# Raw pieces of w_in by half the rows, and five buffers for q, k and v, in a kernel of attention, a dense layer and a mixture of experts

## The chip, the cores and the metric

The kernel runs on one core of a Trainium2 chip. The metric is the time of one execution on the device, in microseconds (us). TensorE (PE) multiplies, VectorE (DVE) and ScalarE (ACT) work on elements, GpSimd (POOL) does small things and indirect transfers, SyncE (SP) issues the other transfers, all on one queue, which 16 DMA engines serve.

## The reference

```
attn = softmax(mask(q @ k^T / 8))            # 4 batches, 8 heads, 576 rows, blocks of 64, float32
x    = (attn @ v), heads side by side        # 2304 tokens x 512
h    = x @ w_in                              # w_in 512 x 2048
x    = where(h > 0, h, exp(min(h, 0)) - 1) @ w_out   # w_out 2048 x 512
do   = x @ w_skip > 0                        # else the token goes out unchanged
e    = argmax(x @ w_gate); g = softmax(x @ w_gate)[e]     # 8 experts
out  = x + g * (relu(x @ w1[e]) @ w2[e])     # w1 512 x 1024, w2 1024 x 512 each
```

w_in and w_out come as 64-bit floats; the kernel reads them as pairs of 32-bit integers and makes 32-bit floats of them itself.

## The kernel before

A recorder (class `Recorder`) takes down every operation of attention, of the dense layer and of the preparation of weights as a step with an engine and an estimated duration. Its function `order` then puts all steps in one order, by dependencies, by free buffers and by those estimates, and every engine's program is issued in that order. So a change of a buffer count or of a load's dependencies moves instructions on all engines. In a profile nearly all of them carry line 310, the recorder's; tiles tell them apart.

Attention is worked through by batch, group, head pair and block of 64 rows: `load_raw` fetches 128 rows (or the last 64) of q, k or v for all heads into a tile `raw` (256 KB, runs of 256 bytes); `prep_k`, `prep_q` and `prep_v` split it into two 16-bit halves (ACT makes the high one, DVE the low one) and transpose it. For the first two tiles of batch 0 PE transposes (tile `tp`), later the DMA does (`DMA_TRANSPOSE`). Scores `s` go to PSUM, DVE takes the maximum (`mx`), ACT the exponential (`e`, with its sum `su`), ACT and DVE split it (`ehl`), it is transposed (`et`), and PE multiplies with `vt` (`xps`). For the scale of v a batch is also read flat (`vflat`, 1152 KB), squared on ACT with a sum (into `col`), and the maximum is taken over partitions with a transpose on PE (`bm`, `bmt`).

The dense layer takes chunks of 256 tokens, `c` = 0 to 8. Chunks 0 and 1 use w_in and w_out in 32 bits (`twi`, `two`; products `h` and `y`, activation `g`), the others the 16-bit halves (`win`, `wout`). Block `j` of 256 columns of w_in is one tile `twi` of 1024 elements in each partition. It comes in two raw pieces of 512 KB, `x = 2j + m` in `raw_load`: piece `m` holds 128 of the 256 columns for all 512 rows, four runs of 1 KB in each partition. `conv` makes floats of a piece with three DVE passes (a TENSOR_SCALAR and two SCALAR_TENSOR_TENSOR), writing four stretches of 128 elements in each partition. The pieces 16 to 31 are of w_out, 128 whole rows each, one run of 4 KB in a partition. A product h of a block needs both pieces of the block.

The buffers of `raw` are a ring: the fourth load has to wait until the tile of the first has been split. The recorder knows that and places loads accordingly. Behind the ninth chunk come the blocks of the experts, from about 580 us on; neither w_in nor raw occurs there.

Of the kernel before, what the change touches and what calls it, by code (L numbers as in the profile page):

```python
# [9 lines left out]
F32 = mybir.dt.float32  # L10
# [337 lines left out]
def tile_kernel(ctx, tc, q, k, v, w_in, w_out, w_skip, w_gate, w1, w2, out):  # L348
    nc = tc.nc
    B, H, S, D = q.shape  # L350
# [101 lines left out]
    w_in32 = w_in.bitcast(I32)  # L452
# [7 lines left out]
    def raw_load(x):  # L460

        if not RING:
            RING.append(True)
            RFREE.extend((99, pool.tile([128, 1024], I32, tag=tag, bufs=bufs, name="rw")) for pool, tag, bufs in ((mo, "pay", 2), (mo, "pay", 2), (wp, "wt", 1)))
            RFREE.extend((16 + 2 * i, wp.tile([128, 1024], I32, tag=f"wo{i}", bufs=1, name="rw")) for i in range(8))
        ok = [r for r in RFREE if r[0] > x]
        if not ok:
            return False
        place = min(ok, key=lambda r: r[0])
        RFREE.remove(place)  # L470
        RAWW[x] = place
        j, m = divmod(x % 16, 2)
        if x < 16:
            f0 = j * 256 + m * 128
            src = w_in32[:, 2 * f0:2 * (f0 + 128)].rearrange("(k p) x -> p k x", p=128)
            dst = place[1].rearrange("p (k x) -> p k x", k=4)
        else:
            r0 = j * 256 + m * 128
            src = w_out32[r0:r0 + 128, :]
            dst = place[1]  # L480
        rc.sync.dma_start(out=dst, in_=src)
        if x - 4 in CONV:
            rc.steps[-1][4].add(CONV[x - 4])
        return True

    def conv(x):

        j, m = divmod(x % 16, 2)
        kind = "wi" if x < 16 else "wo"
        if m == 0:  # L490
            TW[kind, j] = wp.tile([128, 1024], I32, tag=f"{kind}{j}", bufs=1, name=f"t{kind}{j}")
        t = TW[kind, j]
        place = RAWW.pop(x)
        RFREE.append(place)
        raw = place[1].rearrange("p (f two) -> p f two", two=2)
        lo, hi = raw[:, :, 0], raw[:, :, 1]
        if kind == "wi":
            dst = t.rearrange("p (k f) -> p k f", k=4)[:, :, m * 128:(m + 1) * 128]
            lo, hi = (a.rearrange("p (k f) -> p k f", k=4) for a in (lo, hi))
        else:  # L500
            dst = t[:, m * 512:(m + 1) * 512]
        rc.vector.tensor_scalar(out=dst, in0=hi, scalar1=0x07FFFFFF, scalar2=3, op0=ALU.bitwise_and, op1=ALU.logical_shift_left)
        rc.vector.scalar_tensor_tensor(out=dst, in0=hi, scalar=-(1 << 30), in1=dst, op0=ALU.bitwise_and, op1=ALU.bitwise_or)
        rc.vector.scalar_tensor_tensor(out=dst, in0=lo, scalar=29, in1=dst, op0=ALU.logical_shift_right, op1=ALU.bitwise_or)
        CONV[x] = len(rc.steps) - 1
# [97 lines left out]
    ap = rc.pool(at.enter_context(tc.tile_pool(name="attn", bufs=1)))  # L603
# [56 lines left out]
    def trows(n):  # L660
        return 128 if n < 4 else 64

    def load_raw(nm, b, n):
        src = {"q": q, "k": k, "v": v}[nm]
        r = trows(n)
        t = ap.tile([128, H, D], F32, tag="raw", bufs=3, name="raw")
        rc.sync.dma_start(out=t[0:r], in_=src[b, :, n * 128:n * 128 + r, :].rearrange("h p d -> p h d"))
        RAW[nm, b, n] = t

# [555 lines left out]
    def L(nm, b, n):  # L1225
        return lambda: load_raw(nm, b, n)
# [60 lines left out]
    def load_to(n):  # L1287
        while nraw[0] < min(n, 32) and raw_load(nraw[0]):
            nraw[0] += 1

    def conv_step():
        x = nload[0]
        load_to(x + 1)
        conv(x)
        load_to(min(nraw[0] + 2, x + 5))
        nload[0] += 1
# [19 lines left out]
    VF = [4, 5, 6, 6, 7, 8, 9]  # L1316
    rc.base = -300
    load_raw("k", 0, 0)
    load_raw("q", 0, 0)
    load_to(2)  # L1320
    load_raw("k", 0, 1)
# [237 lines left out]
    for i in range(2):  # L1559
        t = wp.tile([128, 2, PW], F32, tag=f"wo{i + 4}", bufs=1, name=f"gp{i}")  # L1560
# [391 lines left out]
```

## Time and profile before

| what | us |
|---|---|
| three runs | 742.56, 750.12, 752.17 |
| median | 750.12 |
| profiled execution | 746.02 |
| its span, first to last instruction | 743.9 |

The page gives busy times of each engine over the span, a row of slices, the DMA queues, the chain of work that ended last and the costliest groups of instructions. Busy times of engines overlap. Windows give the same sums for a stretch; in them the granted clock of PE is a mean, 1.00 for 2.4 GHz throughout and 0.50 for 1.2 GHz throughout. The DMA share is the sum of the packets' times over 16 engines, and passes 1 where packets of one engine overlap. The timeline gives start, duration, instruction, and in brackets the idle time ahead and what ended it.

### The profile page before, as it was taken

Reading aid. Unit: us, or ns where it says so; the run is one execution under the profiler, and the core shown is the slowest. Engines: PE = TensorE matmul, PEld = TensorE weight load, DVE = VectorE, ACT = ScalarE, POOL = GpSimd, SP = SyncE. Lnnn points to the kernel's source line nnn. Section 1 sums busy time; section 2 is a strip of 40 time slices with the busy share of each in tenths; the row PEclk is TensorE's granted clock in tenths of the full one; section 3 lists DMA queues with packets and bytes.
Section 4 is the critical chain, followed back from the end, with each engine's and each line's share of the span. In section 5 each row is a group of like instructions: output and inputs, shape, how many; then the busy total and the mean of one; then the engine's idle time right before and its main releaser. Section 6 shows DMA issues by size and latency. Waiting matters only on the chain.

```text
span 743.9 us, 17734 instructions
## 1 busy us (share of the span) xinstructions
PE 679.4 (91%) x6665; PEld 466.1 (63%) x6665; DVE 578.7 (78%) x1664; ACT 513.9 (69%) x1090; POOL 83.4 (11%) x122
## 2 busy tenths in 40 slices
PE   4689997999999899999999999989999989997894
PEld 3467543775476657657657658657575768675673
DVE  5987989897899797989869966999687634554752
ACT  5876656999797785788758846775365727685782
POOL 2000000010000100000100010100113124143211
PEclk9669999899999999999999999999999999999998
DMA  9999999967787989699656559726267486799941
GB/s 271 270 262 294 292 280 207 203 119 149 145 170 147 172 177 198 122 172 195 112 90 135 90 96 281 277 78 207 57 199 211 124 180 138 200 244 252 272 127 16
DMA packets 267355, 134.52 MB, mean 181 GB/s; under 512 B 234539, under 2 KB 243765, under 8 KB 266736
## 3 DMA queue, kind: packets, MB, share of 16 engines
q1 hardware_dynamic: 263056, 125.69, 72.7%
q0 software_dynamic: 4192, 7.49, 4.7%
q8 instruction: 57, 0.93, 0.5%
q14 instruction: 50, 0.41, 0.2%
HBM read 74.38 MB, written 12.75 MB: 117 GB/s over the span
## 4 chain that ended last, share of the span: by engine, by line
PE 45%; DMA 19%; issue 16%; DVE 12%; ACT 3%; POOL 2%; SPq 1%; POOLq 0%; another core or an unknown queue 0%; DVEq 0%; ACTq 0%
PE h L310 18%; PE y L310 17%; DMA et<-ehl 6%; DMA gp<-pay_d,lists 5%; PE s L310 4%; PE xps L310 3%; DVE ehl L310 2%; DMA rw<-in_moe_w_out_dram 2%; DMA out_dram<-o,gp 2%; DVE two L310 1%; DVE mx L310 1%; DMA vflat<-in_v_dram 1%; POOL out_dram L1684 1%; DMA lst_d<-li,si 1%; DVE el L310 1%
## 5 line engine op out<-in xcount | busy, mean ns | idle before, releaser
L310 PE MATMUL h<-xt,win 128*128 128x256 f16 x1344 | 158.7, 273 | 2.2 <-DVE el L310 2.1
L310 PE MATMUL y<-wout,g 128*128 128x512 f16 x672 | 155.1, 379 | 0.0
L310 PEld LDWEIGHTS <-win 128*128 128x128 f16 x1344 | 128.6, 98 | 23.9 <-issue 2.7
L310 PEld LDWEIGHTS <-g 128*128 128x128 f16 x672 | 63.4, 98 | 68.0 <-issue 1.4
L310 ACT ACTIVATE e<-s,mx 128x512 f32<-128x512 f32 (+4 forms) x160 | 82.2, 516 | 21.4 <-DVE ehl L310 11.5
L310 ACT ACTIVATE ehl<-e,su 128x512 f16<-128x512 f32 (+4 forms) x160 | 79.8, 549 | 13.0 <-DVE su L310 7.5
L310 DVE SCALAR_TENSOR_TENSOR ehl<-e,su,ehl 128x512 f16<-128x512 f32 (+4 forms) x160 | 81.1, 538 | 2.7 <-ACT ehl L310 2.7
L310 DVE TENSOR_REDUCE mx<-s 128x1 f32<-128x512 f32 (+4 forms) x160 | 74.3, 475 | 10.0 <-PE s L310 9.3
L310 PE MATMUL s<-kt,qt 128*128 128x384 f16 (+5 forms) x384 | 68.9, 310 | 9.6 <-ACT e L310 7.9
L310 PE MATMUL xps<-et,vt 128*64 128x128 f16 (+1 forms) x1440 | 51.5, 220 | 14.2 <-DMA et<-ehl 8.2
L310 PEld LDWEIGHTS <-vt 128*64 128x64 f16 x1440 | 41.1, 115 | 35.5 <-issue 22.9
L310 PE MATMUL h<-xt,twi 128*128 128x256 f32 x256 | 62.1, 396 | 0.8 <-DVE g L310 0.8
L310 PE MATMUL y<-two,g 128*128 128x512 f32 x128 | 61.0, 615 | 1.9 <-DVE two L310 1.9
L310 ACT ACTIVATE g<-el,col 128x512 f16<-128x512 f32 x56 | 40.1, 717 | 29.6 <-DVE el L310 29.3
L310 PEld LDWEIGHTS <-p 128*128 128x128 f16 x984 | 47.8, 99 | 14.5 <-issue 6.1
L310 PEld LDWEIGHTS h<-xt,twi 128*128 128x128 f32 x256 | 49.2, 198 | 8.0 <-DVE g L310 1.2
L310 ACT ACTIVATE el<-h,col 128x512 f32<-128x512 f32 x56 | 38.2, 683 | 15.5 <-PE h L310 13.9
L310 DVE SCALAR_TENSOR_TENSOR g<-el,col,g 128x512 f16<-128x512 f32 x56 | 41.6, 744 | 3.5 <-ACT g L310 3.3
L1511 DVE SCALAR_TENSOR_TENSOR p<-p,n,p 128x1024 f16<-128x1024 f32 x32 | 40.7, 1280 | 4.4 <-ACT p L1510 4.2
L310 PEld LDWEIGHTS <-qt 128*128 128x128 f16 (+1 forms) x384 | 27.6, 104 | 26.2 <-issue 12.4
L310 DVE SCALAR_TENSOR_TENSOR el<-h,col,el 128x512 f32<-128x512 f32 x56 | 41.8, 746 | 1.2
L310 DVE TENSOR_TENSOR hh<-r,hh 128x256 f16<-128x256 f32 x36 | 14.8, 422 | 35.0 <-ACT hh L310 35.0
(233 smaller groups left out, 1143.6 us busy)
## 6 DMA issues: line engine op xcount, KB each, us to landing
p<-in_moe_w_dram SPq DMA_DIRECT2D x49, 512.0 KB, 6.1
rw<-in_moe_w_in_dram SPq DMA_DIRECT2D x16, 512.0 KB, 6.2
rw<-in_moe_w_out_dram SPq DMA_DIRECT2D x16, 512.0 KB, 6.3
pb<-in_moe_w_dram SPq DMA_DIRECT2D x10, 512.0 KB, 4.5
vflat<-in_v_dram SPq DMA_DIRECT2D x4, 1152.0 KB, 6.7
out_dram<-pay SPq DMA_DIRECT2D x18, 256.0 KB, 2.8
pay_d<-pay SPq DMA_DIRECT2D x18, 256.0 KB, 2.7
raw<-in_k_dram SPq DMA_DIRECT2D x16, 256.0 KB, 3.6
```

Source lines behind the costliest of these rows:

```text
L310: rec.call(e, time, lambda: getattr(self.real, op)(*args, **kw), reads, writes, dma)
L1511: rc.call("dve", 1.2, lambda: nc.vector.scalar_tensor_tensor(out=half(1), in0=raw.t, scalar=sc, in1=half(0), op0=ALU.mult, op1=ALU.subtrac ...
L1684: i = nc.gpsimd.indirect_dma_start(out=out.rearrange("n (h d) -> (n h) d", h=m), out_offset=bass.IndirectOffsetOnAxis(ap=ts, axis=0), in_= ...
```

## The change

Two things change. A raw piece of w_in holds half the rows (256) and all 256 columns of a block: two runs of 2 KB in each partition, and `conv` writes one stretch of 512 elements, as for w_out. And the ring of `raw` has five buffers where it had three.

```diff
--- before.py
+++ after.py
@@ -471,9 +471,8 @@
         RAWW[x] = place
         j, m = divmod(x % 16, 2)
         if x < 16:
-            f0 = j * 256 + m * 128
-            src = w_in32[:, 2 * f0:2 * (f0 + 128)].rearrange("(k p) x -> p k x", p=128)
-            dst = place[1].rearrange("p (k x) -> p k x", k=4)
+            src = w_in32[256 * m:256 * m + 256, 512 * j:512 * j + 512].rearrange("(k p) x -> p k x", p=128)
+            dst = place[1].rearrange("p (k x) -> p k x", k=2)
         else:
             r0 = j * 256 + m * 128
             src = w_out32[r0:r0 + 128, :]
@@ -494,11 +493,7 @@
         RFREE.append(place)
         raw = place[1].rearrange("p (f two) -> p f two", two=2)
         lo, hi = raw[:, :, 0], raw[:, :, 1]
-        if kind == "wi":
-            dst = t.rearrange("p (k f) -> p k f", k=4)[:, :, m * 128:(m + 1) * 128]
-            lo, hi = (a.rearrange("p (k f) -> p k f", k=4) for a in (lo, hi))
-        else:
-            dst = t[:, m * 512:(m + 1) * 512]
+        dst = t[:, m * 512:(m + 1) * 512]
         rc.vector.tensor_scalar(out=dst, in0=hi, scalar1=0x07FFFFFF, scalar2=3, op0=ALU.bitwise_and, op1=ALU.logical_shift_left)
         rc.vector.scalar_tensor_tensor(out=dst, in0=hi, scalar=-(1 << 30), in1=dst, op0=ALU.bitwise_and, op1=ALU.bitwise_or)
         rc.vector.scalar_tensor_tensor(out=dst, in0=lo, scalar=29, in1=dst, op0=ALU.logical_shift_right, op1=ALU.bitwise_or)
@@ -663,7 +658,7 @@
     def load_raw(nm, b, n):
         src = {"q": q, "k": k, "v": v}[nm]
         r = trows(n)
-        t = ap.tile([128, H, D], F32, tag="raw", bufs=3, name="raw")
+        t = ap.tile([128, H, D], F32, tag="raw", bufs=5, name="raw")
         rc.sync.dma_start(out=t[0:r], in_=src[b, :, n * 128:n * 128 + r, :].rearrange("h p d -> p h d"))
         RAW[nm, b, n] = t
 
```

The recorder plans anew, and the order changes from the second microsecond on up to the first expert blocks; the set of instructions stays the same but for the shapes of the w_in passes. Three places follow. Names end in a buffer number at times; `raw`, `rw` (a raw piece), `twi` and `vflat` are as above.

First place, the start of the program. On SP before (behind its first branch):

```order
L310 DMA raw<-in_k_dram 128x8x64
L310 DMA raw<-in_q_dram 128x8x64
L310 DMA rw<-in_moe_w_in_dram 128x4x256 x2
L310 DMA raw<-in_k_dram 128x8x64
L310 DMA vflat<-in_v_dram 128x2304
L310 DMA raw<-in_q_dram 128x8x64
L310 DMA raw<-in_v_dram 128x8x64
L310 DMA rw<-in_moe_w_in_dram 128x4x256 x2
L310 DMA raw<-in_v_dram 128x8x64
L310 DMA rw<-in_moe_w_in_dram 128x4x256 x2
L310 DMA raw<-in_k_dram 128x8x64
```

On SP now:

```order
L310 DMA raw<-in_k_dram 128x8x64
L310 DMA raw<-in_q_dram 128x8x64
L310 DMA rw<-in_moe_w_in_dram 128x2x512 x2
L310 DMA raw<-in_k_dram 128x8x64
L310 DMA raw<-in_q_dram 128x8x64
L310 DMA vflat<-in_v_dram 128x2304
L310 DMA raw<-in_v_dram 128x8x64 x2
L310 DMA rw<-in_moe_w_in_dram 128x2x512 x2
L310 DMA raw<-in_k_dram 128x8x64
L310 DMA raw<-in_q_dram 128x8x64
L310 DMA rw<-in_moe_w_in_dram 128x2x512
```

The second load of q stands ahead of vflat now, both loads of v stand together, and the third k and q stand ahead of the fifth piece of w_in. On ACT, from the copies of the first transposed q on, before:

```order
L310 ACTIVATE qt<-tp 128x1024 x2
L310 ACTIVATE k_161<-raw 128x8x64
L310 ACTIVATE e_177,su<-s,mx 128x128
L310 ACTIVATE e_182,su<-s,mx 128x128
L310 ACTIVATE vflat,col<-vflat 128x2304
L310 ACTIVATE qq<-raw 128x8x64
L310 ACTIVATE ehl<-e_177,su 128x128
L310 ACTIVATE ehl<-e_182,su 128x128
L310 ACTIVATE e_203,su<-s,mx 128x128
L310 ACTIVATE qt<-tp 128x1024 x2
L310 ACTIVATE vt<-raw,col 128x8x64
L310 ACTIVATE et<-tp 128x512
```

On ACT now:

```order
L310 ACTIVATE qt<-tp 128x1024 x2
L310 ACTIVATE k_161<-raw 128x8x64
L310 ACTIVATE e_177,su<-s,mx 128x128
L310 ACTIVATE qq<-raw 128x8x64
L310 ACTIVATE e_182,su<-s,mx 128x128
L310 ACTIVATE qt<-tp 128x1024
L310 ACTIVATE ehl<-e_177,su 128x128
L310 ACTIVATE qt<-tp 128x1024
L310 ACTIVATE vflat,col<-vflat 128x2304
L310 ACTIVATE ehl<-e_182,su 128x128
L310 ACTIVATE e_187,su<-s,mx 128x256
L310 ACTIVATE e_203,su<-s,mx 128x128
```

The split of the second q (`qq<-raw`) and both copies of its transposes stand ahead of the square of vflat. The splits of v (`vt`) have moved back.

Second place, the seventh to tenth pieces of w_in on SP. Before, from the third k on:

```order
L310 DMA raw<-in_k_dram 128x8x64
L310 DMA wg_79<-in_moe_w_gate_dram 128x4x8
L310 DMA vflat<-in_v_dram 128x2304
L310 DMA raw<-in_q_dram 128x8x64
L310 DMA raw<-in_v_dram 128x8x64
L310 DMA rw<-in_moe_w_in_dram 128x4x256
L310 DMA_TRANSPOSE kt<-k_194 128x8x128
L310 DMA rw<-in_moe_w_in_dram 128x4x256
L310 DMA raw<-in_k_dram 64x8x64
L310 DMA rw<-in_moe_w_in_dram 128x4x256
L310 DMA_TRANSPOSE qt<-qq 128x8x128
L310 DMA rw<-in_moe_w_in_dram 128x4x256
```

On SP now, up to the tenth piece:

```order
L310 DMA_TRANSPOSE qt<-qq 128x8x128
L310 DMA raw<-in_v_dram 64x8x64
L310 DMA rw<-in_moe_w_in_dram 128x2x512
L310 DMA raw<-in_k_dram 128x8x64
L310 DMA wg_79<-in_moe_w_skip_dram 128x4x1
L310 DMA raw<-in_v_dram 128x8x64
L310 DMA qt<-qt 64x1024 x2
L310 DMA_TRANSPOSE kt<-k_215 128x8x64
L310 DMA rw<-in_moe_w_in_dram 128x2x512
L310 DMA_TRANSPOSE qt<-qq 128x8x64
L310 DMA raw<-in_q_dram 128x8x64
L310 DMA rw<-in_moe_w_in_dram 128x2x512 x2
```

Between the seventh and the tenth piece stood a half load of k (64 rows); now a full k, v and q of a later tile stand there, and the transfers of the third tile's k and q have moved ahead.

Third place, DVE at the reduction over the four maxima of v (`col<-col`), among the passes over the sixth and seventh block of w_in (`twi_310`, `twi_313`). Before:

```order
L310 SCALAR_TENSOR_TENSOR g<-g,h 128x512
L310 TENSOR_SCALAR twi_310<-rw 128x4x128
L310 SCALAR_TENSOR_TENSOR twi_310<-rw,twi_310 128x4x128 x2
L310 SCALAR_TENSOR_TENSOR g<-g,h 128x512
L310 TENSOR_REDUCE col<-col 128x1
L310 TENSOR_SCALAR twi_310<-rw 128x4x128
L310 SCALAR_TENSOR_TENSOR twi_310<-rw,twi_310 128x4x128
L310 SCALAR_TENSOR_TENSOR g<-g,h 128x512
L310 SCALAR_TENSOR_TENSOR twi_310<-rw,twi_310 128x4x128
L310 TENSOR_SCALAR twi_313<-rw 128x4x128
```

On DVE now:

```order
L310 SCALAR_TENSOR_TENSOR twi_310<-rw,twi_310 128x512 x2
L310 TENSOR_REDUCE mx<-s 128x1 x2
L310 SCALAR_TENSOR_TENSOR g<-g,h 128x512
L310 TENSOR_SCALAR twi_310<-rw 128x512
L310 SCALAR_TENSOR_TENSOR twi_310<-rw,twi_310 128x512
L310 TENSOR_SCALAR su<-su 128x2
L310 SCALAR_TENSOR_TENSOR twi_310<-rw,twi_310 128x512
L310 RECIPROCAL su<-su 128x2
L310 TENSOR_SCALAR twi_313<-rw 128x512
L310 SCALAR_TENSOR_TENSOR twi_313<-rw,twi_313 128x512
L310 TENSOR_REDUCE col<-col 128x1
L310 SCALAR_TENSOR_TENSOR twi_313<-rw,twi_313 128x512
```

The reduction stood right behind a g; now two reductions of scores, five passes over w_in and two small steps of a softmax stand between that place and the reduction.

## Rows read from the trace of the kernel before

**Rows 1.** The page: span, and busy time of PE (its first part).
```profile
span 743.9 us, 17734 instructions
...
PE 679.4 (91%) x6665; PEld 466.1 (63%) x6665; DVE 578.7 (78%) x1664; ACT 513.9 (69%) x1090; POOL 83.4 (11%) x122
```

**Rows 2.** Windows by stage: length, busy us (instructions) by engine, clock, DMA share, GB/s.
```profile
0.00:140.00 140.00, 109.75 (x716) 72.34 (x717) 119.41 (x321) 96.66 (x209) 4.56 (x41) 0.87 1.08 265
140.00:580.00 440.00, 430.06 (x4010) 285.38 (x4009) 371.40 (x1108) 315.88 (x693) 32.83 (x48) 1.00 0.71 157
```

**Rows 3.** Windows of the first 140 us, columns PE, PEld, DVE, ACT, POOL, clock, DMA.
```profile
0.00:20.00 20.00, 9.03 (x83) 6.62 (x84) 12.19 (x40) 12.21 (x20) 3.79 (x38) 1.00 1.01 276
20.00:40.00 20.00, 12.04 (x111) 8.96 (x109) 18.36 (x54) 17.52 (x50) 0.00 (x0) 0.59 1.12 271
40.00:60.00 20.00, 17.68 (x99) 13.64 (x98) 17.66 (x40) 15.81 (x31) 0.35 (x1) 0.73 1.14 250
60.00:140.00 80.00, 71.00 (x426) 43.11 (x426) 71.20 (x190) 51.12 (x111) 0.41 (x2) 0.94 1.08 264
```

**Rows 4.** Windows of w_in packets, of w_out packets, of q, k, v and transposes.
```profile
65.50:68.40 2.90, 2.39 (x12) 1.76 (x10) 1.66 (x4) 2.62 (x5) 0.00 (x0) 1.00 1.10 348
77.50:79.40 1.90, 1.90 (x10) 1.68 (x9) 1.01 (x5) 1.87 (x6) 0.00 (x0) 1.00 1.00 399
...
54.60:56.00 1.40, 1.40 (x8) 1.24 (x7) 1.40 (x3) 0.85 (x2) 0.00 (x0) 1.00 1.31 251
```

**Rows 5.** DMA packets by size, first from 65.5 to 68.4, then 77.5 to 79.4.
```profile
DMA packets 1018, 1.01 MB, mean 348 GB/s; under 512 B 32, under 2 KB 1018, under 8 KB 1018
...
DMA packets 215, 0.76 MB, mean 399 GB/s; under 512 B 30, under 2 KB 30, under 8 KB 215
```

**Rows 6.** DMA issues from 5.4 to 6.5 us: KB, us to landing.
```profile
raw<-in_q_dram SPq DMA_DIRECT2D x1, 256.0 KB, 8.6
```

**Rows 7.** Timeline of SP, ACT and PE, the second q and its surroundings.
```profile
5.48 0.78 SPq L310 DMA_DIRECT2D raw<-in_q_dram  x1
...
11.32 0.37 ACT L310 ACTIVATE e<-s,mx 128x128 f32<-128x128 f32 x1 [0.67 <-DVE mx L310]
...
12.88 2.12 ACT L310 ACTIVATE vflat<-vflat 128x2304 f32<-128x2304 f32 x1 [0.30 <-DMA vflat<-in_v_dram]
...
15.00 0.61 ACT L310 ACTIVATE qq<-raw 128x512 f16<-128x512 f32 x1
...
16.49 2.03 PE L310 MATMUL tp<-id,qq 128*128 128x128 f16 x24 [0.44 <-DVE qq L310]
```

**Rows 8.** Waits of DVE in the first 20 us: us in total, times, longest.
```profile
DVE bmt L310 <- PE bm L310: 1.5, 1, 1.5
```

**Rows 9.** Timeline of DVE and ACT around the fourth vflat.
```profile
60.93 0.43 DVE L310 TENSOR_SCALAR twi<-rw 128x512 int32<-128x512 int32 x1 [0.41 <-DMA rw<-in_moe_w_in_dram]
...
64.32 2.12 ACT L310 ACTIVATE vflat<-vflat 128x2304 f32<-128x2304 f32 x1 [2.34 <-DMA vflat<-in_v_dram]
...
66.57 0.16 DVE L310 TENSOR_REDUCE col<-col 128x1 f32<-128x4 f32 x1 [3.17 <-ACT vflat L310]
```

**Rows 10.** Waits of DVE (0 to 140 us) and of PE (60 to 140).
```profile
DVE two L310 <- DMA rw<-in_moe_w_out_dram: 2.3, 4, 1.1
...
DVE twi L310 <- DMA rw<-in_moe_w_in_dram: 1.6, 2, 1.1
...
PE y L310 <- DVE two L310: 1.9, 2, 1.0
...
PE h L310 <- DVE g L310: 0.8, 1, 0.8
```

**Rows 11.** Instructions on the raw pieces: ns minimum/median/maximum, first and last start.
```profile
L310 DVE SCALAR_TENSOR_TENSOR twi<-rw,twi x32: 671/685/698, 9.2 to 73.3; 128x512 int32<-128x512 int32 x32
L310 DVE SCALAR_TENSOR_TENSOR two<-rw,two x32: 680/684/704, 72.7 to 120.6; 128x512 int32<-128x512 int32 x32
L310 SPq DMA_DIRECT2D rw<-in_moe_w_in_dram x16: 507/743/3832, 1.9 to 61.9; - x16
...
L310 SPq DMA_DIRECT2D rw<-in_moe_w_out_dram x16: 345/578/1982, 64.2 to 113.9; - x16
```

## The prediction

> **What bounds the kernel now.** I read the page first: TensorE (PE) is busy for 679.4 of 743.9 us [rows 1]. That share is a mean over stages, so the windows by stage come next [rows 2]. From 140 to 580 us PE works 430.06 of 440 us at the full granted clock: 9.9 us at most can be had there. From 580 us on neither part of the change has any work, and the instructions stand in the same order as before. What is left is 0 to 140 us: PE is busy for 109.75 us of it and idle for 30.3, VectorE (DVE) is busy for 119.41 (85%), and the share of the 16 DMA engines is 1.08 (packet times summed, so a full queue).
>
> Inside that stretch [rows 3] PE's idle time lies early: 11.0 us in the first 20 us, 8.0 in the next 20, 2.3 in the third, 9.0 in the last 80. From 20 to 60 us the granted clock is 0.59 and 0.73 on average, so PE spends part of that time at 1.2 GHz, after it idled for more than half of the first 20 us. DVE is busy for 18.36 of 20 us by then. So the engines first wait for the first loads and for each other; from 20 us on DVE is the narrow one, with a full DMA queue beside it; from 140 us on it is PE.
>
> **Part one: half the rows, all columns.** Each of the 16 pieces of w_in is 512 KB as before, but 256 runs of 2 KB where it was 512 runs of 1 KB. What that does to the queue is bounded by two stretches [rows 4, 5]. From 65.5 to 68.4 us nearly all packets are 1 KB ones of w_in (986 of 1018), and they move 348 GB/s. From 77.5 to 79.4 us most are 4 KB ones of w_out (185 of 215), at 399 GB/s. No row has w_in in packets of 2 KB. The 16 pieces are 8.39 MB: 24.1 us at the first rate, 21.0 at the second, so the gain in queue time is between 0 and 3.1 us. If a packet has a fixed cost, the two rates (2.874 and 2.506 us per MB) give 2.63 us per MB at 2 KB, and 22.1 us for the pieces: 2.0 us less by the end of the sixteenth, 0.13 each. I take that, since 2 KB lies between the two.
>
> The Trainium skill, "DMA: Bandwidth & Descriptors", section Specifications, says that a transfer of 512 B or more runs at line rate. By that rule 1 KB runs are long enough, this part gives nothing, and the sum below would end at 748.3 us and not at 747.5. The two stretches, which differ by 15% at 1 KB and 4 KB, speak against it.
>
> Of the 2.0 us only what an engine waits for counts. DVE waits 2.3 us in all for landed w_out pieces and 1.6 for w_in [rows 10]. That reaches PE only where PE stood behind DVE: 0.8 us at h and 1.9 at y [rows 10]. The first lies behind w_in pieces: I take it. The second I leave, for in the new order DVE has made five passes over w_out by the eighth g where it had made eight, so three passes of 0.68 us [rows 11] come 2.1 us later there. This term lies between a gain of 2.7 us and a loss of 2.1; I take a gain of **0.8**, the wait nearest to w_in.
>
> The DVE passes handle the same 512 elements, in one run where there were four. A pass over w_out, which has one run already, takes a median of 684 ns against 685 for w_in [rows 11]: nothing. SyncE (SP) takes a median of 743 ns to issue a w_in piece and 578 for w_out [rows 11]. Half of that gap, 16 times, would be 1.3 us of SP's time; SP mostly waits for buffers and PE for other things, so I take nothing, with bounds 0 and 1.3.
>
> **Part two: five buffers.** No instruction is added. Loads move ahead, and with them the planned order of everything up to 580 us. The clear place is the first 20 us [rows 6, 7]. Before, q of tile 1 is issued at 5.48 us, behind the 1152 KB load of v (vflat), and lands 8.6 us later, at 14.1. ScalarE (ACT) starts to split it at 15.00, behind the square of vflat that starts at 12.88, and PE starts its transposes at 16.49. Now q is issued ahead of vflat, and its split stands ahead of the square. 1152 KB (1.18 MB) at 399 GB/s are 3.0 us, so q can land at about 11.1 us; ACT has one exp in front, from 11.32 on for 0.37 us [rows 7], so the split can start near 11.7, or 3.3 us earlier. Not all of that lasts, because what follows hangs on DVE, which is at 92% from 20 us on. What lasts is the idle time of DVE that gets filled, nearest the 1.5 us in front of the maximum over v (bmt) [rows 8], ahead of which reductions and ehl passes stand now, and a little of the gaps between. I take **1.8** us, with bounds 0 (all swallowed) and 3.3. The cover on the other side: the square of v comes later, and so do the scale and the v tiles that need it, behind exp and ehl work on ACT. Were that work not enough, the first xps products would wait for v and the 1.8 us shrink to nothing.
>
> The second place is at 66.57 us, where a reduction of the maxima of v on DVE waits 3.17 us for ACT, and ACT 2.34 us for the fourth vflat [rows 9]. In the new order eight rows (nine instructions, about 4 us by the busy times of their like) stand in front of that reduction that stood behind it, while the load stands one w_in piece further back (512 KB at 348 GB/s, 1.5 us). So the stall should be mostly covered. What it cost PE is the 0.8 us at h that is counted already.
>
> Moving q, k and v ahead puts 256-byte packets in front of w_in. Such a stretch moves 251 GB/s [rows 4]: a 256 KB load costs 1.04 us of the queue. The eighth to tenth w_in pieces now stand behind about four full loads more, 4.2 us. DVE comes to these pieces later too, since attention passes moved ahead of the conversions; I take nothing here and keep the 4.2 us for the range.
>
> **Sum.** The profiled execution took 746.0 us (span 743.9, and 2.1 around it). Less 1.8 and 0.8 that is 743.4. It lies 4.1 us below the median of the three runs shown, 750.1; the same gain from the median gives **747.5 us**, which I predict.
>
> **The rivals.**
> *Slower: late w_in pieces.* At 60.93 us DVE had no slack: it waited 0.41 us for a piece of w_in to land [rows 9]. If the eighth to tenth pieces come 4.2 us late and DVE has nothing else in front, the conversions, h and g behind them move by as much and the filled gaps are lost: 750.1 + 4.2 = 754.3 us. It decides from the point where the delay exceeds the attention work that now stands ahead of those conversions on DVE; three ehl passes and their reductions are about 4 us, which is why I hold it the less likely.
>
> *No difference.* DVE fills 85% of the stretch and PE 89% from 60 us on [rows 3]. A head start of 1.8 us may end as a longer wait of PE for a converted block or of DVE for exp, and the pieces may gain queue time only: 750.1 us.
>
> *More: the clock.* PE is busy for 29.7 us from 20 to 60 us [rows 3]. At the full clock these would be 0.59 x 12.0 + 0.73 x 17.7 = 20.0 us. If a denser start lets the clock rise early, up to 9.7 us come on top: 737.8 us. Against it: DVE at 92% feeds PE in this stretch and stays as it is.
>
> **Numbers.** Chances: the forecast, a gain of 1 to 7 us, 0.50; no difference 0.20; late pieces 0.17; clock 0.13. The new order from 140 to 580 us adds a scatter of its own, a few of the 9.9 us of idle either way. The range from 738 to 755 leaves out the far end of the clock case and the tail of the late pieces, under 2 in 10 together; the forecast's own range is 743 to 749. Over 2% is 15 us, about what a measurement of this kernel can tell from no change. Faster by that needs the whole clock gain and most of the idle before 60 us: 0.05. Slower by that needs late pieces at several places: 0.03. Within it: 0.92.
>
> **What would show it.** Right: PE's transposes of the second q start near 13 us and not at 16.5; the waits for bmt and for the maxima of v are gone from DVE; stretches of w_in packets alone move about 380 GB/s; the first fp16 h products come 2 to 4 us earlier and the rest runs as before. Wrong: DVE waits longer than 1.6 us for w_in; PE's idle time from 140 to 580 us changes by more than the 2.6 us of the sum; the granted clock from 20 to 60 us differs by more than a tenth.

## The result and the profile after

The changed kernel takes 737.92 us (median of 20 runs, 734.57 to 743.36) against 745.40 us for the kernel before (20 runs, 741.23 to 752.70): a ratio of **0.9916**, 95% interval 0.9893 to 0.9939. Ratios compare fast runs with fast runs, so this one is not the quotient of the two medians. It is a gain of 4.5 to 8.0 us, within 2% and in the direction that I forecast, but 1.7 to 3.1 times the 2.6 us of my sum. The 737.92 us lies at the lower end of my range (738 to 755) and below the forecast's own 743 to 749. My 747.5 us was too high for a second reason: the median of three runs on which I put the gain, 750.1, lay 4.7 us above that of twenty. The sum against the profiled execution, 743.4, used the better base.

The page of the changed kernel, span and busy times, beside [rows 1]:

```profile
span 737.0 us, 17736 instructions
...
PE 675.2 (92%) x6665; PEld 464.0 (63%) x6665; DVE 576.2 (78%) x1664; ACT 511.8 (69%) x1090; POOL 84.9 (12%) x122
```

The windows of after, with the columns of [rows 2, 3]: length, busy us by engine from PE to POOL, granted clock, DMA share, GB/s.

```profile
0.00:140.00 140.00, 108.00 (x771) 69.16 (x772) 117.56 (x318) 94.69 (x208) 4.96 (x43) 0.96 1.03 259
140.00:580.00 440.00, 430.70 (x4002) 289.62 (x4000) 373.47 (x1121) 318.84 (x699) 32.84 (x46) 1.00 0.76 159
```

```profile
0.00:20.00 20.00, 9.08 (x82) 6.31 (x83) 10.07 (x32) 11.75 (x21) 3.79 (x38) 1.00 0.99 264
20.00:40.00 20.00, 12.98 (x123) 9.20 (x122) 18.84 (x59) 18.77 (x52) 0.00 (x0) 0.96 0.93 233
40.00:60.00 20.00, 15.14 (x92) 11.22 (x88) 15.28 (x36) 14.86 (x31) 0.35 (x1) 0.87 1.08 260
60.00:140.00 80.00, 70.80 (x484) 42.43 (x483) 73.36 (x193) 49.31 (x108) 0.82 (x4) 0.98 1.06 264
```

PE's idle time looks as before: 32.0 us in the first 140 us (30.3 before) and 9.3 in the next 440 (9.9 before). But instructions cross such borders when an order changes. A border that PE's products don't cross is the start of the first product of the experts, `ahp`: in all kernels of this study the same 4712 products stand ahead of it. I call that moment the **end of the body**. The order behind it is not the same at once: in the changed kernel PE's products differ from those of before up to 598 us, and in some kernels below up to 685 us, so 580 us was too early a border in my prediction. Windows up to it, first of before, then of after:

```profile
0.00:579.37 579.37, 539.19 (x4712) 357.10 (x4713) 490.61 (x1427) 411.91 (x899) 37.29 (x88) 0.97 0.80 183
```

```profile
0.00:576.20 576.20, 534.90 (x4712) 355.00 (x4713) 488.90 (x1428) 410.65 (x899) 37.70 (x88) 0.99 0.82 183
```

The body ends 3.2 us earlier. PE is idle for 40.2 us of it before and 41.3 after, so the gain is not in its waits: its busy time is 4.3 us shorter. Two more executions of each order, described below, say the same: 538.2 and 539.4 us busy and 41.2 and 39.9 idle in the order of before, 533.3 and 534.3 busy and 39.9 and 41.0 idle in the new one. The rest of the difference between the two spans, 3.7 us, lies behind the body. There three executions of the order of before took 164.5, 172.6 and 174.8 us, and three of the new order 160.8, 163.9 and 170.2, so a single execution says nothing about that tail.

The places of which the prediction spoke. PE, the second q and what follows it, timeline of after (start, duration, instruction, idle time ahead and what ended it):

```profile
13.70 2.03 PE L310 MATMUL tp<-id,qq 128*128 128x128 f16 x24
...
24.66 0.42 PE L310 MATMUL xps<-et,vt 128*64 128x128 f16 x4
...
46.67 1.03 PE L310 MATMUL h<-xt,twi 128*128 128x256 f32 x4
```

ACT and DVE of after in the same stretch:

```profile
16.89 2.12 ACT L310 ACTIVATE vflat<-vflat 128x2304 f32<-128x2304 f32 x1
...
16.12 0.35 DVE L310 SCALAR_TENSOR_TENSOR ehl<-e,su,ehl 128x128 f16<-128x128 f32 x1 [1.54 <-ACT ehl L310]
...
17.48 0.90 DVE L310 TENSOR_REDUCE mx<-s 128x1 f32<-128x256 f32 x2 [1.02 <-PE s L310]
```

The transposes start at 13.70 us where they started at 16.49 [rows 7], as forecast. The square of `vflat` starts at 16.89 where it started at 12.88 [rows 7], and the first products with v come at 24.66 us; before they came at 20.73. DVE is busy for 10.07 of the first 20 us where it was busy for 12.19 [rows 3]. Its wait of 3.17 us for the maxima of v at 66 us [rows 9] is gone, as forecast. The first h product comes at 46.67 us, 0.8 us earlier than the 47.46 of before.

The longest waits of DVE from 0 to 140 us in after, in us, times and longest, beside [rows 8, 10]:

```profile
DVE twi L310 <- DMA rw<-in_moe_w_in_dram: 6.6, 6, 3.4
DVE ehl L310 <- ACT ehl L310: 3.5, 4, 1.5
...
DVE two L310 <- DMA rw<-in_moe_w_out_dram: 1.5, 2, 1.1
```

The longest of them, and SP in after where the piece for it is issued:

```profile
60.48 0.43 DVE L310 TENSOR_SCALAR twi<-rw 128x512 int32<-128x512 int32 x1 [3.35 <-DMA rw<-in_moe_w_in_dram]
```

```profile
49.54 2.08 SPq L310 DMA_TRANSPOSE qt<-qq  x1
52.51 3.62 SPq L310 DMA_TRANSPOSE et<-ehl  x1
56.18 0.58 SPq L310 DMA_DIRECT2D rw<-in_moe_w_in_dram  x1
```

The same piece, the eleventh, on SP before:

```profile
43.94 0.52 SPq L310 DMA_DIRECT2D rw<-in_moe_w_in_dram  x1
```

The piece stands behind a transpose that takes SP 3.62 us to issue, and it lands 4.3 us after its own issue. So the rival of late w_in pieces was right that such waits would come: 1.6 us of them before [rows 10], 6.6 now. They are not at the pieces that it named. The eighth to tenth were issued 9 to 13 us later than before, and no wait for them shows; 5.2 of the 6.6 us are waits for the eleventh to thirteenth and the fifteenth, from 60 to 73 us.

### The profile page after: what moved, and what is told of

Read it like the earlier page. It is cut to its first block, busy times and chain, and to the rows that moved or that the text cites. A ratio compares the mean times of both kernels' runs of the same rounds, so it can differ in the third digit from the quotient of the medians.

```text
span 737.0 us, 17736 instructions
## 1 busy us (share of the span) xinstructions
PE 675.2 (92%) x6665; PEld 464.0 (63%) x6665; DVE 576.2 (78%) x1664; ACT 511.8 (69%) x1090; POOL 84.9 (12%) x122
## 5 line engine op out<-in xcount | busy, mean ns | idle before, releaser
L310 PE MATMUL h<-xt,twi 128*128 128x256 f32 x256 | 59.4, 383 | 3.9 <-DVE g L310 2.4
L310 PE MATMUL xps<-et,vt 128*64 128x128 f16 (+1 forms) x1440 | 49.5, 218 | 13.8 <-DVE xt L310 2.8
L310 PEld LDWEIGHTS <-vt 128*64 128x64 f16 x1440 | 39.9, 113 | 32.2 <-issue 23.8
L310 PEld LDWEIGHTS h<-xt,twi 128*128 128x128 f32 x256 | 47.4, 190 | 10.8 <-DVE g L310 3.0
L310 PEld LDWEIGHTS <-hh 128*64 128x64 f16 (+1 forms) x432 | 28.5, 106 | 19.6 <-DVE hh L310 2.6
```

The source lines that it names most:

```text
L310: rec.call(e, time, lambda: getattr(self.real, op)(*args, **kw), reads, writes, dma)
```

## The experiments

Every ratio is to the kernel before, run on the same chip beside it; 1 us is 0.0013. Body ends are those of single profiled executions.

**One part alone.** `rows_only` has 2 KB runs and three buffers:

```diff
-        t = ap.tile([128, H, D], F32, tag="raw", bufs=5, name="raw")
+        t = ap.tile([128, H, D], F32, tag="raw", bufs=3, name="raw")
```

> The kernel before with part one alone (half rows, all columns); every engine has the order of before. Theory A (packets of 2 KB save queue time, and little of it is waited for): ratio 0.997 to 1.000, that is 0 to 2 us; DVE waits for w_in and w_out landings together 3 us or less where they were 3.9. Rival (part one makes the whole gain): ratio near 0.992. Rival by the Trainium skill, DMA: Bandwidth & Descriptors, Specifications (512 B is enough): ratio 1.000, stretches of w_in packets alone at 348 GB/s.

Measured: 1.0013 (0.9981 to 1.0045); the body ends at 579.37 us, as before. Its order is that of before on all engines, so it isolates the runs. The same stretch as in [rows 4, 5], now in 2 KB packets; window, then packets by size:

```profile
65.50:68.40 2.90, 2.90 (x15) 2.41 (x15) 2.05 (x5) 1.87 (x4) 0.00 (x0) 1.00 1.05 386
```

```profile
DMA packets 579, 1.12 MB, mean 386 GB/s; under 512 B 32, under 2 KB 32, under 8 KB 579
```

386 GB/s where 1 KB packets gave 348: the queue is faster, as I had worked out (380). (The same stretch in `before_again`, below, shows 363, with 16 packets of 4 KB among its 1011.) DVE's waits did not shrink with it: 1.7 us for w_in and 2.6 for w_out, 4.3 together where I had expected 3 or less and where 3.9 stood before [rows 10]. That the body ends at the very time of before is chance in part: near 500 us this execution was 1.5 us ahead, and it lost that from there on (last section).

`bufs5_only` is the kernel before with five buffers alone; it has 1 KB runs and the order of the changed kernel:

```diff
-        t = ap.tile([128, H, D], F32, tag="raw", bufs=3, name="raw")
+        t = ap.tile([128, H, D], F32, tag="raw", bufs=5, name="raw")
```

> The kernel before with part two alone (five buffers); every engine has the order of the changed kernel. Theory B (the new order makes the gain, from 200 us on and behind 580 us, while late w_in pieces take back the start): ratio 0.990 to 0.995, and DVE waits for w_in in the first 140 us are 6.6 us or more, since 1 KB packets come later still. Rival (the parts need each other): ratio 0.998 or more.

Measured: 0.9948 (0.9914 to 0.9982), body end 575.37 us; DVE waits 5.9 us for w_in, less than I had expected. `after_again` is the changed kernel once more, beside it:

> The changed kernel once more, for a second trace and a ratio on the chip of the two parts. All theories: ratio 0.989 to 0.994. If the 3.4 us that the first trace shows between the first block of experts and the end are chance, this trace shows another figure there; if they belong to the change, 2 us or more again.

Measured: 0.9903 (0.9870 to 0.9936), body end 573.19 us. The tail behind the body took 163.9 us, 0.6 less than in the first trace of before, so the 3.4 us of the first trace were chance. The gain needs the order that the five buffers bring. Whether the runs add something in the new order (0.0045 between the two) stays open, since the intervals overlap. Two profiles of the changed kernel end the body 3.0 us apart; `before_again`, a second profile of the kernel before, ends it at 579.39 us, 0.02 from the first.

> The kernel before once more, for a second trace. If the granted clock of 0.59 and 0.73 from 20 to 60 us belongs to its order, it shows again; if it is chance, it is above 0.85. The stretch from the first block of experts (579.4 us) to the end took 164.5 us: the same within 1 us if it belongs to the order.

The clock showed again: 0.60 from 20 to 40 us and 0.71 from 40 to 60. The stretch to the end took 172.6 us, 8 us more, so it does not belong to the order.

Two runs of the new order show what that clock is worth, and how its column has to be read. Windows from 20 to 40 us, and the xps products in them, of `bufs5_only`, then of `after_again`; last the xps of `bufs5_only` behind 60 us:

```profile
20.00:40.00 20.00, 13.33 (x122) 9.36 (x120) 18.87 (x60) 18.77 (x51) 0.00 (x0) 1.00 0.98 238
L310 PE MATMUL xps<-et,vt x54: 265/314/316, 24.3 to 39.7; 128*64 128x128 f16 x54
```

```profile
20.00:40.00 20.00, 13.33 (x122) 9.33 (x121) 18.90 (x60) 18.76 (x52) 0.00 (x0) 0.50 0.95 231
L310 PE MATMUL xps<-et,vt x54: 263/313/316, 24.2 to 39.6; 128*64 128x128 f16 x54
```

```profile
L310 PE MATMUL xps<-et,vt x60: 219/219/243, 61.1 to 94.4; 128*64 128x128 f16 x60
```

The column says 1.00 for the one and 0.50 for the other, but a product takes the same 314 and 313 ns (median) in both, and 219 ns at the full clock behind 60 us. So both ran that stretch at 1.2 GHz. The trace of `bufs5_only` has its first record of the clock at 50.4 us, and the column counts the time ahead of a first record as 1.00. The 1.00 of the first 20 us of before [rows 3] is of that kind: its first record is at 20.3 us, and the transposes ahead of it take 314 ns (median), as long as those at 0.50 behind it (311).

The clock did differ a little later. The first h products of the same order, in after, where the record shows 1.00 from 45.2 us on, and in `bufs5_only`:

```profile
46.67 1.46 PE L310 MATMUL h<-xt,twi 128*128 128x256 f32 x6
49.63 4.58 PE L310 MATMUL h<-xt,twi 128*128 128x256 f32 x20 [1.51 <-ACT xt L310]
```

```profile
46.98 2.77 PE L310 MATMUL h<-xt,twi 128*128 128x256 f32 x6
50.06 4.11 PE L310 MATMUL h<-xt,twi 128*128 128x256 f32 x17 [0.31 <-ACT xt L310]
```

Six products took 1.31 us less at the full clock. Both then waited for the same `xt` from ACT, and the next product started 0.43 us earlier, of which 0.31 had been there before: nearly all that the clock gave back went into a longer wait.

**The second q behind vflat again.** `q_behind_vflat` is the changed kernel, in which the load of the second q takes its place in the plan just behind that of vflat:

```diff
+    qld = len(rc.steps) - 1
     vflat(0)
+    vld = next(i for i in range(qld + 1, len(rc.steps)) if rc.steps[i][0] == "sp")
+    rc.steps[qld][3] = rc.steps[vld][3] + 0.5
```

> The changed kernel (2 KB runs, five buffers) with one load moved back: the second q stands behind the 1152 KB load of v again, as before the change; everything is planned anew from there. By the prediction's largest term (the second q earlier is worth 1.8 us) the transposes of the second q go back from 13.7 to about 16.5 us, the body up to the first expert product ends 1.8 us later than in the changed kernel (573.2 and 576.2 us in its two profiles, so about 575 to 578), and the time is near 741 us (ratio to before 0.994). By the rival, that the gain is made by the later batches' loads and not by the start, nothing moves: ratio 0.991, body end 573 to 576 us.

Measured: 1.0057 (1.0017 to 1.0098), body end 585.14 us, 9 to 12 us later than the changed kernel. PE's transposes of the second q in it:

```profile
16.98 2.03 PE L310 MATMUL tp<-id,qq 128*128 128x128 f16 x24 [0.44 <-DVE qq L310]
```

The place moved as intended, and the time by 11 us where the place was priced at 1.8. But everything behind was planned anew: the first h stands at 46.84 us, the loss is not there; by the first fp16 h it is 5.6 us (213.54 against 207.98). It is the loss of a whole plan, and the price of the place cannot be read from it. It also shows that five buffers alone bring no gain.

**Which loads the buffers serve.** In `five_first` only the 15 loads of batch 0 use five buffers freely, in `five_later` only the 45 loads of batches 1 to 3; the others also wait for the split three places earlier. Added to the planner's `order`, here for `five_first` (`x < 15` for the other):

```diff
+        for (_, tag), tiles in self.rings.items():
+            if tag == "raw":
+                for x in range(3, len(tiles)):
+                    if x >= 15:
+                        own = set(self.users.get(tiles[x][0], ()))
+                        for i in own:
+                            if not steps[i][4] & own:
+                                steps[i][4] |= set(self.users.get(tiles[x - 3][0], ()))
```

> The changed kernel, in which only the 15 loads of q, k and v of batch 0 use the five buffers freely; every later load also waits until the load three places before it has been split, as with three buffers. If the gain comes from the start (batch 0), it all stays: ratio to before about 0.991, first expert product at 573 to 576 us. If it comes from batches 1 to 3, whose loads run further ahead, it goes: ratio near 1.000, first expert product near 579.4 us.

Measured: 1.0004 (0.9973 to 1.0034), body end 581.49 us.

> The counterpart: the 15 loads of batch 0 wait as with three buffers, the 45 loads of batches 1 to 3 use five. The start (first 20 us) is in the order of before: transposes of the second q at 16.5 us, DVE waits 1.5 us for bmt. If the gain comes from the start it goes: ratio near 1.000 and first expert product at 579 us. If it comes from the later batches it stays: ratio 0.991, 573 to 576 us. If both runs with a part of the ring keep the gain, the ring's length is not its cause, and the order in which the old plan stood was itself the slow one.

Measured: 0.9970 (0.9942 to 0.9998), body end 579.41 us. Neither keeps the gain. If one half carries any of it, it is the later one, 2.2 us by the ratio; but each of the two is a new plan as well.

**Late w_in pieces.** `w_in_ahead` is the changed kernel with pieces loaded further ahead of their conversion:

```diff
-        load_to(min(nraw[0] + 2, x + 5))
+        load_to(min(nraw[0] + 2, x + 9))
```

> The changed kernel, in which raw pieces of w_in may be loaded up to nine pieces ahead of the conversion where it was five, so that the eighth to tenth piece stand ahead of the DMA transposes of the third k and q. If the late pieces of the changed kernel (DVE waits 6.6 us for them, longest 3.4) cost time, DVE's wait for w_in falls below 2 us, the first y product comes at about 80 us again (83.7 in the changed kernel, 80.4 before) and the time falls by 1 to 3 us against the changed kernel: ratio to before 0.987 to 0.990. If the wait is idle time of DVE that nothing hangs on in the end, the wait goes and the time stays: 0.991.

Measured: 0.9926 (0.9893 to 0.9960), body end 576.73 us. DVE's waits for w_in in it:

```profile
DVE twi L310 <- DMA rw<-in_moe_w_in_dram: 1.4, 2, 1.0
```

The wait fell from 6.6 to 1.4 us and the first y came at 77.25 us, 6.5 us earlier than in the changed kernel; the body ended no earlier. By the first h of the second chunk the lead was a lag (138.19 us against 134.64). So taking DVE's long waits for w_in away brought nothing that shows in the end. That they cost nothing in the changed kernel is not shown by it: this is another plan, and plans differ by more than these waits (next).

**Ring or plan.** Each change so far set up a new plan, so two plans were compared each time and not one cause. The last four kernels plan the same work with one assumption of the planner moved by some per cent, with three buffers and with five:

```diff
-    LAT = {"pe": 0.2, "dve": 0.23, "act": 0.23, "pool": 0.13, "sp": 1.0, None: 0.0}
+    LAT = {"pe": 0.2, "dve": 0.23, "act": 0.23, "pool": 0.13, "sp": 1.05, None: 0.0}
```

In `three_n1` and `five_n1` it is this line; in `three_n2` and `five_n2` the numbers of dve and act are 0.24 and sp stays 1.0.

> 2 KB runs, three buffers, and one number of the planner moved: the latency that it assumes for a transfer is 1.05 us instead of 1.00. The start of SP's program stays as before the change, what follows is planned anew (3083 of 18486 places on PE hold another instruction than before the nudge). If the ring of five makes the gain, this plan ends like the one of before: ratio 1.000 within 0.003, first expert product at 579.4 us within 1.5. If the gain is that one plan came out better than another, by chance, it may lie anywhere in the 573 to 585 us that the plans so far covered, and the two kernels of three buffers can be as fast as those of five.

> 2 KB runs, three buffers, and another number moved: the latency assumed between VectorE or ScalarE and other engines is 0.24 us instead of 0.23. Ring theory: ratio 1.000 within 0.003, first expert product at 579.4 us within 1.5, and above both kernels of five buffers. Scatter of plans: anywhere from 573 to 585 us, with no order between three and five.

> The changed kernel with the first nudge (assumed latency of a transfer 1.05 us). The start of SP's program stays that of the changed kernel up to its thirteenth load. Ring theory: ratio 0.991 to 0.995 as with the plan of the changed kernel, first expert product at 573 to 576 us, 3 us or more ahead of the same nudge with three buffers. Scatter of plans: anywhere from 573 to 585 us.

> The changed kernel with the second nudge (0.24 us between VectorE or ScalarE and other engines). Ring theory: ratio 0.991 to 0.995, first expert product at 573 to 576 us, 3 us or more ahead of the same nudge with three buffers. Scatter of plans: anywhere from 573 to 585 us.

Measured, with all others, the stall (below) in us, and body ends of the profiled execution, or of each where there are two:

| kernel | buffers, batch 0 / later | ratio (interval) | body end, us | stall near 500 us |
|---|---|---|---|---|
| before | 3 / 3 | 1 | 579.37, 579.39 | 2.1, 2.0 |
| rows_only | 3 / 3 | 1.0013 (0.9981 to 1.0045) | 579.37 | 2.0 |
| three_n1 | 3 / 3 | 1.0070 (1.0037 to 1.0103) | 584.61 | 3.2 |
| three_n2 | 3 / 3 | 1.0029 (0.9988 to 1.0070) | 581.08 | 2.1 |
| five_first | 5 / 3 | 1.0004 (0.9973 to 1.0034) | 581.49 | 2.1 |
| five_later | 3 / 5 | 0.9970 (0.9942 to 0.9998) | 579.41 | 1.0 |
| changed kernel | 5 / 5 | 0.9916, 0.9903 | 576.20, 573.19 | 1.0, 1.0 |
| bufs5_only | 5 / 5 | 0.9948 (0.9914 to 0.9982) | 575.37 | 1.0 |
| w_in_ahead | 5 / 5 | 0.9926 (0.9893 to 0.9960) | 576.73 | 1.0 |
| five_n1 | 5 / 5 | 1.0029 (0.9997 to 1.0061) | 578.46 | 0 |
| five_n2 | 5 / 5 | 1.0016 (0.9983 to 1.0049) | 578.86 | 1.0 |
| q_behind_vflat | 5 / 5 | 1.0057 (1.0017 to 1.0098) | 585.14 | 1.0 |

Two things follow. A nudge that should be worth nothing moves the time by up to 0.6% with three buffers (1.0070 against 1.0013) and by 1.2% with five (1.0029 against the mean of 0.9916 and 0.9903), as much as the whole gain. Of the five plans with five buffers throughout, the changed kernel's and that of `w_in_ahead` are faster than before; the other three, two of them nudges that move an assumed latency by 4 or 5%, are not. And in each of the three pairs that differ by the ring alone (no nudge, first, second) five buffers are ahead: by 1.0%, 0.4% and 0.1% in time (0.9910 from the two ratios against 1.0013, and so on), by 4.5 (the mean of three executions of that order), 6.2 and 2.2 us at the end of the body. Only the first of these differences in time is clear of its intervals, and the 2.2 us lie within the 3.0 by which two executions of one order differ. So the three pairs suggest some 4 us for the ring, with a scatter of plans as large; they don't show it.

**One wait that goes with the ring.** The last column separates the kernels without exception: 1.0 us or none where the later batches have five buffers, 2.0 to 3.2 where they have three. PE near 500 us, in front of an h product of a late chunk; timeline of before, of `three_n1` and of after:

```profile
499.75 1.47 PE L310 MATMUL h<-xt,win 128*128 128x256 f16 x12 [2.12 <-DVE el L310]
```

```profile
503.32 4.45 PE L310 MATMUL h<-xt,win 128*128 128x256 f16 x24 [3.15 <-DVE rts L310]
```

```profile
496.57 2.79 PE L310 MATMUL h<-xt,win 128*128 128x256 f16 x24 [0.98 <-DVE n L310]
```

DVE makes the activation of the dense layer and prepares expert weights (`p`) there. In before four passes like the first of these rows stand between 492 and 499 us, ahead of the `el` that PE's next products hang on; DVE's timeline of before:

```profile
492.03 1.28 DVE L1511 SCALAR_TENSOR_TENSOR p<-p,n,p 128x1024 f16<-128x1024 f32 x1
...
497.70 1.28 DVE L1511 SCALAR_TENSOR_TENSOR p<-p,n,p 128x1024 f16<-128x1024 f32 x1
...
498.96 0.74 DVE L310 SCALAR_TENSOR_TENSOR el<-h,col,el 128x512 f32<-128x512 f32 x1
```

Where the later batches have five buffers, attention is over sooner: the last of the 384 products s comes at 415.6 to 427.6 us in their eight profiled executions, and at 428.2 to 432.6 us in the six with three. That the earlier end of attention is what shortens the stall was not tried by itself. Nor is the shorter stall the gain: PE's idle time in the body is the same in both orders (39.9 to 41.2 and 39.9 to 41.3 us, three executions each), so other waits make up for it, and `q_behind_vflat` and both nudged kernels of five buffers have the short stall without the gain. What the changed kernel has less of is busy time of PE.

## Why the prediction was right and wrong

**Faster queue through 2 KB runs: right. Its 0.8 us: not shown.** I took 380 GB/s and 386 was measured in the stretch that moved 348 [rows 4]. SP's median time to issue a piece fell too, from 743 ns [rows 11] to 604, most of the gap to w_out (578). The step that failed is "the first lies behind w_in pieces: I take it": PE's 0.8 us wait at h [rows 10] was for `g` from DVE, behind the reduction that waited for ACT [rows 9], and DVE's own wait for w_in stayed (1.7 us). In `before_again`, the same kernel, that wait of PE is not there at all, so it was no base for a price. The ratio of this part alone, 1.0013, lies between 1.4 us faster and 3.4 slower. By the Trainium skill, "DMA: Bandwidth & Descriptors", section Specifications, a transfer of 512 B or more runs at line rate, so longer runs would give nothing. For the time of this part alone that came true within the interval. For the rate it did not: the same stretch of the same order moved 348 GB/s in 1 KB packets and 386 in 2 KB packets.

**Second q earlier: the place right, the 1.8 us not shown.** The transposes came 2.8 us earlier (I had worked out up to 3.3), and DVE's wait for `bmt` fell from 1.5 to 0.6 us. What failed is the cover that I named myself: the square of v came 4.0 us later, and the first xps products with it, 3.9 us later. DVE idled for 2.1 us more in the first 20 us than before, in new waits for ACT and PE. The first h was 0.8 us ahead, the first y 3.3 us behind (83.73 us against 80.41). The first fp16 h, for which I had named 2 to 4 us, came 0.4 us earlier (207.98 against 208.42; 206.59 in `after_again` and 208.64 in `bufs5_only`). `five_first`, which starts with the same loads in the same order, is not faster than before.

**Late w_in pieces: the waits came, at other pieces, and the price is not shown.** I gave it 0.17 and 4.2 us. DVE's waits for w_in grew by 5.0 us. They came at the eleventh to thirteenth and the fifteenth piece and not at the eighth to tenth, and at the longest the piece was late on SP already: issued 12 us later than before, behind a transpose that took 3.62 us to issue, it landed 4.3 us after that. With the waits gone the body ended no earlier in `w_in_ahead`, but that is another plan. The row on which I relied, a DVE without slack at 60.93 us [rows 9], showed a wait and not what waits behind it.

**The clock: a wrong price.** I valued busy time at a low granted clock as if all of it would come off the time. At the first h products it does not: of 1.31 us that six products save, 0.12 is left at the next. The 737.8 us of that rival lie next to the measured median by chance. Of my signs of error, the clock from 20 to 60 us did differ by more than a tenth by its column (0.96 and 0.87 against 0.59 and 0.73). From 20 to 40 us most of that is the column: the changed kernel's first record is at 34.9 us, and its xps up to 40 us take 314 ns (median), as at 0.50. From 40 to 60 us the difference is real: the full clock came at 45.2 us where it came at 51.0 before.

**"The rest runs as before": the step that failed most.** I counted places up to 140 us and gave the plan from 140 to 580 us "a scatter of its own, a few of the 9.9 us of idle". That idle time did stay (9.3 us). The scatter is in the whole body, and it is larger: it ends between 573 and 585 us in ten plans of the same work. Of the 4.3 us of PE's busy time that the new plan saves, products with w_in in 32 bits make 2.7 (62.1 us before, 59.4 after; 60.5 in `after_again`) and xps 2.0 (51.5 and 49.5), and other groups are some longer; groups overlap where PE turns from one to the other, so these don't add up. Part of the 2.7 is the clock that rose earlier: the first eight of these products took 3.72 us before, at 634 ns each for most of them, and in after they took 379 ns each for most. Where the rest comes from stays open.

So the verdict (within 2%, somewhat faster) came out as forecast, by luck more than by the sum: both mechanisms were seen at work, neither of their two terms is shown in the time, and plans of the same work with five buffers came out from 1% faster to 0.6% slower. Why this plan is one of the faster ones stays open.

## What to carry to other kernels

Where a change passes through a planner, the plan itself is a draw: before pricing single places, plan the same work with an assumption moved by a few per cent, and don't take a gain below that scatter for the worth of the change, since it may be a good draw. A wait that a trace shows is worth something only with the name of what is queued behind it; here the body got shorter beside 5 us of new DVE waits, and a stall of PE that is 1 us shorter left its idle time as it was. Hold a granted clock of 1.00 against the duration of a product before you build on it. And take the base from as many runs as there are: the median of three runs was off by 4.7 us, more than the gain that I forecast.

## What the runs showed of the hardware

Run length still counts between 1 and 4 KB: loads of the weights moved 348 GB/s at 1 KB [rows 4], 386 at 2 KB (`rows_only`, the same stretch) and 399 at 4 KB [rows 4, another stretch].

In before PE's clock was at its lower level, 1.2 GHz, ahead of 20 us: the transposes there take 314 ns (median), as at 0.50. A short rise aside, the full clock came at 51.0 us in before, and at 45.2, 49.1 and 50.4 us in three executions of the new order: the moment differs by 5 us in one and the same order.

Behind the stall near 500 us the clock can fall again. Windows of the first products after it, of before (stall 2.1 us, 12 products), of `rows_only` (2.0 us, 12 products, the same order) and of `three_n1` (3.2 us, 24):

```profile
499.75:501.22 1.47, 1.47 (x19) 1.33 (x19) 1.47 (x5) 1.47 (x3) 0.00 (x0) 1.00 0.95 238
```

```profile
498.22:500.70 2.48, 2.48 (x19) 1.81 (x18) 2.48 (x6) 2.48 (x5) 0.00 (x0) 0.56 0.98 294
```

```profile
503.32:507.77 4.45, 4.45 (x25) 3.31 (x25) 4.45 (x10) 4.45 (x6) 0.00 (x0) 0.62 0.87 212
```

After the longer stall the clock was at 0.62 on average and 24 products took 4.45 us; in after, behind 0.98 us of idle time, 24 took 2.79. After a stall of 2 us in one and the same order 12 products took 1.47 us in before and 2.48 in `rows_only`, which lost 1.0 of its lead of 1.5 us there. In `three_n2`, behind 2.1 us, it was at 0.72 on average in the next 2.6 us. So a stall of 2 us costs the clock in some executions and not in others, one of 1 us in none of these, and a stall can cost more than its own length: 1.7 us on top of 3.2.
